# Attention beside the last stage ended sooner, and the last products of a seven-product scheme in another order

## Chip, cores and metric

One core of a Trainium2 chip. The metric is the device time of one execution in microseconds (us): the median of 3 runs, with the least and the greatest. Profile times are counted from the start of the profiled span.

## What is computed

Attention over a window, with a few global keys, and then a feed-forward block (ReGLU) on its result. Batch 4, 8 heads, 768 positions, head size 64; the feed-forward block takes 3072 tokens of width 512 through width 1536.

```python
def _attn_ref(q, k, v, n_global, n_local):          # n_global 8, n_local 96
    scores = scale * np.matmul(q, k.transpose(0, 1, 3, 2))
    is_global = pos[None, :] < int(n_global)
    is_local = (rel >= 0) & (rel < int(n_local))
    keep = is_global | is_local
    ...
    scores = np.where(keep, scores + bias, -1000000000.0)
    a = np.exp(scores - np.max(scores, axis=-1, keepdims=True))
    a = a / (np.sum(a, axis=-1, keepdims=True) + 1e-09)
    return np.matmul(a, v)

def _moe_ref(x, w_gate, w_val, w_out):              # x: the attention's result
    gate = np.maximum(x @ w_gate, 0.0)
    val = x @ w_val
    return (gate * val @ w_out).astype(np.float32)
```

## The kernel before

The 3072 tokens are worked in eight halves of 384 (half a batch item each), c = 0 to 7. The feed-forward block of half c and the attention of half c + 1 go through the engines together: the code makes a list of feed-forward items and a list of attention pieces, and `weave` lays the pieces between the items. Every engine takes its own instructions in the order in which the code gives them out.

For half c the feed-forward items are, for each of 12 slices of the width 1536, a gate (4 matmuls, then a ReLU on ScalarE) and a val (4 matmuls, then a product on VectorE, which writes `ht`), and then the output products:

```python
def gate(fc, ...):
    psg = products(f"g{fc % 4}", wg, fc, d0, d1)          # 4 matmuls 128x384, lhsT = wg, rhs = xT
    ...
    nc.scalar.activation(gr, psg[:, 0:QH], AF.Relu, bias=0.0, scale=1.0)

def val(fc, ...):
    psv = products("v", wv, fc, d0, d1)
    ...
    nc.vector.tensor_tensor(ht[:, fc, :], psv[:, 0:QH], st["r", fc], op=ALU.mult)
```

The attention of a half has 30 pieces (some of them empty, called `wait`): three units of scores, each in four PSUM banks, twelve exponentials with masks, and for each of four pairs of heads two AV products (5 matmuls each) with the normalisation: on ScalarE a logarithm `lnd` after each AV and one exponential `rcp` for both, on VectorE two products, which write a quarter of `xT`. The next half's gates read `xT`.

```python
return (X(U[0]) + X() + X() + X() + wait + X(U[1]) + X() + X() + a0[0:1] + X() + a0[1:2] + N(0) + wait
        + X(U[2]) + X() + a1[0:1] + X() + X() + a1[1:2] + N(1) + wait * 2 + AV(2) + N(2) + wait * 2
        + AV(3) + N(3))
```

```python
def spread(items, first, last):
    n = len(items)
    return [(first + (i + 0.5) / n * (last - first), f) for i, (_, f) in enumerate(items)]

for c in range(2, NHALF):                                  # NHALF = 8
    placed = []
    if c + 1 < NHALF:
        placed.append(spread(attention_pieces(c + 1), 0.0, 0.92))
    ...
    f1, f2 = ffn_pieces(c)
    weave(f1 + f2, *placed)
```

The output products of two blocks of 128 tokens are taken together by a scheme of seven half-size products in place of eight (Strassen's, in Winograd's form): `Pair`. Each product is 6 matmuls 128x256. Products 1 to 7 read `ht`, sums of it (`ss`), weights (`bb`) or differences of weights (`tt`); sums on VectorE put the four result blocks together in `obuf`. For c = 6 the items are p1, p2, p4, p6, p5, p7, p3. The very last pair is split differently, so that blocks can be stored one by one:

```python
def p1():                                                  # P1
    self.product(bank("b"), 0, hh(0, 0), bb(0, 0))
    st["o"] = obuf[:, n_results[0] % 2]
    nc.scalar.copy(st["o"][:, 2], st["b"][:, 0:DH])
def p2():                                                  # P2
    self.product(bank("a"), 0, hh(0, 1), bb(1, 0))
def p6():                                                  # o0 = P1 + P2 and o1 = P1 + P6
    self.product(st["a"], DH, ss(2), tt(2))
    add(st["o"][:, 0:2], two(st["a"]), st["o"][:, 2:3].to_broadcast([128, 2, DH]))
def block(t, d, i):                                        # store block i
    store(t, st["o"][:, i : i + 1], d, d + 1)
def onto(i, key, j):                                       # o_i = product + o_j
    add(st["o"][:, i], st[key][:, 0:DH], st["o"][:, j])
def last6():
    p6()
    block(0, 0, 0)
def last4():
    self.product(bank("4"), 0, hh(1, 1), tt(4))
    onto(2, "4", 1)
def last7():
    self.product(bank("7"), 0, ss(3), tt(3))
    onto(2, "7", 2)
    block(1, 0, 2)
    onto(3, "7", 1)
def last5():
    self.product(bank("5"), 0, ss(1), tt(1))
    onto(3, "5", 3)
    block(1, 1, 3)
    onto(4, "5", 1)
def last3():
    self.product(bank("3"), 0, ss(4), bb(1, 1))
    onto(4, "3", 4)
    block(0, 1, 4)
...
    return [(0.65, f) for f in (p1, p2, last6, last4, last7, last5, last3)]
```

PSUM is used through three pools: two banks for AV (and the first bank of each score unit), three for scores, three for the feed-forward products (`ff_ps`).

Of the kernel before, what the change touches and what calls it, by code (L numbers as in the profile page):

```python
# [16 lines left out]
def kernel(  # L17
# [27 lines left out]
    NHALF = 2 * B  # L45
# [450 lines left out]
    def score_unit(s, groups, pools):  # L496


        b, half = divmod(s, 2)
        out = []  # L500
        for pp, g in groups:
            banks = []
            for e in range(2):
                pool, name = pools.pop(0)
                banks.append(pool.tile([128, 512], FP32, name=name))
                out.append((pp, g, e, banks[e]))
            c = 0
            for j, a, w, m in banks_of_half[half][g]:
                for p in (2 * pp, 2 * pp + 1):
                    for e in range(2):  # L510
                        r = slice(64 * e, 64 * e + 64)
                        q3 = qT2[s % 2][r, p].rearrange("d (n p) -> d n p", n=NN)
                        nc.tensor.matmul(banks[e][:, c : c + NN * w], lhsT=kT[b % 2][p][r, j, :],  # L513
                                         rhs=q3[:, :, a : a + w], start=True, stop=True)
                    c += NN * w
        return out

    def unit_exp(s, pp, g, e, ps):
        bank = banks_of_half[s % 2][g]
        cols = sum(2 * NN * w for _, _, w, _ in bank)  # L520
        es = es_pool.tile([128, 480], BF16, name="es")
        nc.scalar.activation(es[:, 0:cols], ps[:, 0:cols], AF.Exp, bias=0.0, scale=scale)  # L522

        def mask():
            c = 0
            for j, a, w, m in bank:
                n_ = 2 * NN * w
                e4 = es[:, c : c + n_].rearrange("k (i n p) -> k i n p", i=2, n=NN)
                h0 = 4 * pp + e
                mk = m_all[:, h0 : h0 + 3 : 2, 0 if j == 0 else 1, :, m : m + w]  # L530
                if w == WQ:
                    e4 = e4.rearrange("k i n p -> k i (n p)")
                    mk = mk.rearrange("k i n p -> k i (n p)")
                nc.vector.tensor_mul(e4, e4, mk)  # L534
                for i in range(2):
                    es_of[s, 2 * pp + i, j, e] = (es, c + i * NN * w)
                c += n_

        return mask

    def attention_pieces(s):
        masks, units = [], []

        def flush():
            for f in masks:
                f()
            masks.clear()

        def scores(groups, pools):
            units.extend(score_unit(s, groups, list(pools)))  # L550

        def x(scored=None):
            ready = masks[:]
            masks.clear()
            if scored:
                scores(*scored)
            masks.append(unit_exp(s, *units.pop(0)))
            for f in ready:
                f()

        U = [([(0, 0), (0, 1)], (AVB, QKB, QKB, QKB)),
             ([(0, 2), (1, 0)], (AVB, QKB, QKB, QKB)),
             ([(1, 1), (1, 2)], (AVB, QKB, QKB, QKB))]
        X = lambda u=None: [(0.0, lambda: x(u))]
        AV = lambda p: [(0.0, lambda e=e: (flush(), piece_av(s, p, e))) for e in range(2)]
        N = lambda p: [(0.0, lambda: piece_norm(s, p, 1))]
        wait = [(0.0, lambda: None)]
        a0, a1 = AV(0), AV(1)
# [4 lines that stand above are left out]
# [30 lines left out]
    class Pair:  # L603
# [31 lines left out]
        def items(self, between=(), split=False):  # L635

            st = {}
            between = dict(between)
            hh = lambda t, f: lambda i: self.h(t, f, i, i + 1)[:, 0]
            ss = lambda n: lambda i: self.s[n][:, i]  # L640
            bb = lambda f, d: lambda i: B(i, i + 1, f, d)[:, 0]
            tt = lambda n: lambda i: T(n, i, i + 1)[:, 0]
            add = lambda o, x, y: nc.vector.tensor_tensor(o, x, y, op=ALU.add)  # L643
            two = lambda ps: ps.rearrange("p (b d) -> p b d", b=2)

            def bank(key):
                st[key] = ff_psum.tile([128, DM], FP32, name="ff_ps")
                return st[key]

            def store(t, blocks, d0=0, d1=2):  # L650
                c, n = self.tiles[t]
                nc.sync.dma_start(out=two(out_v[c, n])[:, d0:d1], in_=blocks)


            def p1():
                self.product(bank("b"), 0, hh(0, 0), bb(0, 0))
                st["o"] = obuf[:, n_results[0] % 2]
                n_results[0] += 1
                nc.scalar.copy(st["o"][:, 2], st["b"][:, 0:DH])

            def p2():
                self.product(bank("a"), 0, hh(0, 1), bb(1, 0))

            def p4():
                self.product(bank("d"), 0, hh(1, 1), tt(4))

            def p6():
                self.product(st["a"], DH, ss(2), tt(2))
                add(st["o"][:, 0:2], two(st["a"]), st["o"][:, 2:3].to_broadcast([128, 2, DH]))

            def p5():
                self.product(st["d"], DH, ss(1), tt(1))
                add(st["o"][:, 2:4], two(st["d"]), st["o"][:, 1:2].to_broadcast([128, 2, DH]))

            def second(ps):
                add(st["o"][:, 1:5:3], ps.unsqueeze(1).to_broadcast([128, 2, DH]), st["o"][:, 2:4])
                store(1, st["o"][:, 1:5:3])

            def p7():
                self.product(bank("c"), 0, ss(3), tt(3))  # L680

            def p3():
                self.product(st["c"], DH, ss(4), bb(1, 1))
                second(st["c"][:, 0:DH])
                add(st["o"][:, 3], st["c"][:, DH:], st["o"][:, 3])
                store(0, st["o"][:, 0:4:3])

            def block(t, d, i):  # L690
                store(t, st["o"][:, i : i + 1], d, d + 1)

            def onto(i, key, j):
                add(st["o"][:, i], st[key][:, 0:DH], st["o"][:, j])

            def last6():
                p6()
                block(0, 0, 0)

            def last4():  # L700
                self.product(bank("4"), 0, hh(1, 1), tt(4))
                onto(2, "4", 1)

            def last7():
                self.product(bank("7"), 0, ss(3), tt(3))
                onto(2, "7", 2)
                block(1, 0, 2)
                onto(3, "7", 1)

            def last5():  # L710
                self.product(bank("5"), 0, ss(1), tt(1))
                onto(3, "5", 3)
                block(1, 1, 3)
                onto(4, "5", 1)

            def last3():
                self.product(bank("3"), 0, ss(4), bb(1, 1))
                onto(4, "3", 4)
                block(0, 1, 4)

            def item(name, f):
                def g():
                    f()
                    for x in between.get(name, ()):
                        x()
                return (0.65, g)

            if split:
                return [(0.65, f) for f in (p1, p2, last6, last4, last7, last5, last3)]
            return [item(*x) for x in (("1", p1), ("2", p2), ("4", p4), ("6", p6), ("5", p5), ("7", p7), ("3", p3))]  # L730

    def ffn_pieces(c):
# [73 lines left out]
# [4 lines that stand above are left out]
# [28 lines left out]
    def AV(s, p, *pools):  # L838
        piece_av_wide(s, p, *pools)
        piece_norm_wide(s, p)  # L840
# [155 lines left out]
    for c in range(2, NHALF):  # L996
        placed = []
        if c + 1 < NHALF:
            placed.append(spread(attention_pieces(c + 1), 0.0, 0.92))
        if c + 2 < NHALF:  # L1000
            load_qk(c + 2, 0, H)
            load_v_half(c + 2)
            placed.append(spread(early_pieces(c + 2), 0.25, 0.75))
        f1, f2 = ffn_pieces(c)
        weave(f1 + f2, *placed)
# [35 lines left out]
```

The softmax here doesn't subtract the row's maximum and nothing guards it: scores larger than these inputs give would overflow.

## Time and profile before

| | |
|---|---|
| time, median of 3 runs | 240.92 us (240.51 to 241.19) |
| span of the profiled run | 239.0 us |
| TensorE (PE) busy | 229.8 us, 96% |
| VectorE (DVE) busy | 173.7 us, 73% |
| ScalarE (ACT) busy | 149.5 us, 63% |
| GpSimd (POOL) busy | 90.3 us, 38% |
| granted TensorE clock | 1.0 |
| bytes read and written in HBM | 28.38 MB and 6.29 MB |

How to read the profile: "L742" is line 742 of the kernel. L742 is a matmul of a gate or val, L632 one of the seven products, L431 of an AV, L513 of scores; L440 is the logarithm and L445 the exponential of the normalisation, L451 its product; L751 is the ReLU, L758 the product that writes `ht`; L522 and L534 are exponential and mask of the scores; L643 is a sum onto `obuf`, L652 a store. A name after the engine is the tile written. The chain of work that ended last is followed back from the last instruction, at each step to what released it; "issue" is time in which an engine waited for nothing that the profile shows. The end of a matmul in the profile is modelled, and matmuls overlap, so what is read here is the distance of their starts. Idle time of an engine that isn't the bottleneck costs nothing.

### The profile page before, as it was taken

To read this page: it belongs to the slowest core of one execution; us is meant where nothing else is said; L and a number is where in the kernel's file an instruction comes from. 1 tells how busy PE (TensorE), PEld (TensorE's weight loads), DVE (VectorE), ACT (ScalarE), POOL (GpSimd) and SP (SyncE) were. 2 spreads that over 40 slices of the span, in tenths; PEclk is the share of its full clock that TensorE was granted. 3 is DMA by queue.
4 is the path that set the end of the run, shared out by engine and by line. 5 is a ranking of instruction groups with operands and counts; after the bars stand their busy time and mean duration, and the time that the engine had idled before them with its cause. 6 is when DMAs were issued, how large, how long until landed. Compare 5 with 4: busy or idle time off the path is not lost.

```text
span 239.0 us, 5383 instructions
## 1 busy us (share of the span) xinstructions
PE 229.8 (96%) x1967; PEld 152.4 (64%) x1967; DVE 173.7 (73%) x443; ACT 149.5 (63%) x324; POOL 90.3 (38%) x191
## 2 busy tenths in 40 slices
PE   6889999999999999999999999999999999999992
PEld 3676656656458566766658566766658666756682
DVE  6878667756778779396866879496866878664783
ACT  6999756568653787657754787657754787433300
POOL 8998804925194067303491066402450000000000
PEclk9999999999999999999999999999999999999999
DMA  6999999997459943928349754919321200020004
GB/s 171 200 181 185 205 290 252 161 101 256 101 167 126 310 101 86 96 90 264 89 59 117 244 162 89 93 56 299 81 54 44 91 0 0 3 88 0 3 27 150
DMA packets 70650, 30.42 MB, mean 127 GB/s; under 512 B 47744, under 2 KB 69248, under 8 KB 70624
## 3 DMA queue, kind: packets, MB, share of 16 engines
q0 software_dynamic: 34896, 10.27, 38.2%
q1 hardware_dynamic: 35728, 19.82, 28.5%
q8 instruction: 15, 0.25, 0.4%
q14 instruction: 11, 0.09, 0.1%
HBM read 28.38 MB, written 6.29 MB: 145 GB/s over the span
## 4 chain that ended last, share of the span: by engine, by line
PE 81%; ACT 6%; DMA 6%; DVE 3%; POOL 1%; issue 1%; SPq 0%; DVEq 0%
PE ff_ps L742 49%; PE ff_ps L632 14%; PE ff_ps L775 9%; PE av_ps L431 5%; DMA wv<-in_moe_w_val_dram 4%; PE av_ps L513 2%; PE qk_ps L513 2%; ACT es L359 2%; DMA qs<-in_q_dram 1%; POOL vbuf L154 1%; ACT obuf L263 1%; ACT lnd L440 1%; DVE obuf L643 1%; DVE xT L451 1%; ACT rcp L445 1%
## 5 line engine op out<-in xcount | busy, mean ns | idle before, releaser
L742 PE MATMUL ff_ps<-xT,wg 128*128 128x384 bf16 x384 | 77.9, 326 | 0.4 <-DVE xT L451 0.4
L742 PE MATMUL ff_ps<-xT,wv 128*128 128x384 bf16 x384 | 77.9, 326 | 0.1
L751 ACT ACTIVATE grelu<-ff_ps 128x384 bf16<-128x384 f32 x96 | 46.8, 490 | 47.2 <-PE ff_ps L742 34.2
L758 DVE TENSOR_TENSOR ht<-ff_ps,grelu 128x384 f16<-128x384 f32 x96 | 53.3, 556 | 27.3 <-PE ff_ps L742 24.0
L742 PEld LDWEIGHTS <-wv 128*128 128x128 bf16 x384 | 36.1, 98 | 24.3 <-issue 1.7
L742 PEld LDWEIGHTS <-wg 128*128 128x128 bf16 x384 | 36.4, 98 | 21.9 <-issue 0.7
L451 DVE TENSOR_TENSOR xT<-av_ps,rcp 64x384 bf16<-64x384 f32 x48 | 26.6, 554 | 22.2 <-ACT rcp L445 21.1
L440 ACT ACTIVATE lnd<-av_ps 64x384 f32<-64x384 f32 x48 | 23.3, 485 | 17.8 <-PE av_ps L431 17.1
L367 POOL CAST kc<-ks 128x384 bf16<-128x384 f32 x20 | 10.2, 553 | 55.5 <-DMA ks<-in_k_dram 48.1
L534 DVE TENSOR_TENSOR es<-es,m_all 128x432 bf16<-128x432 bf16 (+3 forms) x108 | 30.3, 321 | 0.8 <-ACT es L522 0.7
L522 ACT ACTIVATE es<-qk_ps 128x432 bf16<-128x432 f32 (+2 forms) x54 | 27.8, 530 | 0.1
L154 POOL DMA_DIRECT2D vbuf<-in_v_dram x29 | 24.8, 870 | 0.3 <-DVE ht L758 0.3
L775 PE MATMUL ff_ps<-wo_sb,ht 128*128 128x512 f16 x96 | 23.6, 378 | 0.0
L643 DVE TENSOR_TENSOR obuf<-ff_ps,obuf 128x512 f32<-128x512 f32 (+1 forms) x35 | 20.4, 589 | 3.4 <-PE ff_ps L632 0.8
L431 PEld LDWEIGHTS <-vbuf 128*128 128x128 bf16 x216 | 18.3, 98 | 6.7
L431 PE MATMUL av_ps<-es,vbuf 128*128 128x216 bf16 (+4 forms) x216 | 21.4, 226 | 0.0
L632 PEld LDWEIGHTS <-hsum 128*128 128x128 f16 x168 | 16.2, 98 | 1.8
L632 PEld LDWEIGHTS <-ht 128*128 128x128 f16 x144 | 13.8, 98 | 3.4 <-DVE ht L758 0.8
L632 PE MATMUL ff_ps<-wo_sum,hsum 128*128 128x256 f16 x126 | 15.0, 272 | 0.0
L775 PEld LDWEIGHTS <-ht 128*128 128x128 f16 x96 | 8.6, 97 | 8.0 <-issue 0.6
L445 ACT ACTIVATE rcp<-lnd 128x384 f32<-128x384 f32 x24 | 12.5, 523 | 0.8
L632 PE MATMUL ff_ps<-wo_sb,ht 128*128 128x256 f16 x96 | 12.0, 273 | 0.5 <-DVE ht L758 0.5
(130 smaller groups left out, 252.7 us busy)
## 6 DMA issues: line engine op xcount, KB each, us to landing
out_dram<-obuf SPq DMA_DIRECT2D x22, 256.0 KB
ks<-in_k_dram SPq DMA_DIRECT2D x5, 768.0 KB
qs<-in_q_dram SPq DMA_DIRECT2D x5, 768.0 KB
vbuf<-in_v_dram POOLq DMA_DIRECT2D x23, 120.0 KB, 4.7
wv<-in_moe_w_val_dram POOLq DMA_DIRECT2D x3, 512.0 KB, 10.0
wo_sb<-in_moe_w_out_dram POOLq DMA_DIRECT2D x1, 1536.0 KB, 21.7
wg<-in_moe_w_gate_dram POOLq DMA_DIRECT2D x2, 512.0 KB, 10.0
ks<-in_k_dram SPq DMA_DIRECT2D x4, 192.0 KB
```

The costliest lines, as they stand in the source:

```text
L154: nc.gpsimd.dma_start(out=v_dst(b, NG + r0, NG + r0 + n, j), in_=v[b, :, KT * j + r0 : KT * j + r0 + n, :].rearrange("h p d -> p h d"))
L431: nc.tensor.matmul(av3[:, :, a : a + w], lhsT=vb[:, j, z0 : z0 + 128], rhs=es[:, c : c + NN * w].rearrange("k (n p) -> k n p", n=NN), star ...
L440: nc.scalar.activation(ln[o0 : o0 + 64], av[d0 : d0 + 64, 0:QH], AF.Ln, bias=0.0, scale=1.0)
L451: nc.vector.tensor_tensor(xT_of[s][r, p, :], av_of[s, p, e][r, 0:QH], av_of[s, p, "r"][r], op=ALU.mult)
L522: nc.scalar.activation(es[:, 0:cols], ps[:, 0:cols], AF.Exp, bias=0.0, scale=scale)
L534: nc.vector.tensor_mul(e4, e4, mk)
L632: nc.tensor.matmul(ps[:, c0 : c0 + DH], lhsT=lhs(i), rhs=rhs(i), start=(i == 0), stop=(i == NP - 1), skip_group_check=True)
L643: add = lambda o, x, y: nc.vector.tensor_tensor(o, x, y, op=ALU.add)
L742: nc.tensor.matmul(st[key][:, 0:QH], lhsT=w_of(w, dc, fc), rhs=xT_of[c][:, dc, :], start=(dc == 0), stop=(dc == N_DC - 1))
L751: nc.scalar.activation(gr, psg[:, 0:QH], AF.Relu, bias=0.0, scale=1.0)
L758: nc.vector.tensor_tensor(ht[:, fc, :], psv[:, 0:QH], st["r", fc], op=ALU.mult)
L775: nc.tensor.matmul(ps2, lhsT=ht[:, fc, n * 128 : (n + 1) * 128], rhs=wo_sb[:, fc, :], start=(fc == 0), stop=(fc == N_FC - 1))
```

## The change

There are two parts. The first lets the pieces of the last half's attention (c = 6, the attention of half 7) run to 87 per cent of the stage in place of 92; it is to have the normalisations done before the products that follow them. The other stages keep 0.92. The second gives the last pair's products the order 1, 2, 6, 5, 7, 4, 3 and forms P5 + o1 once, for two blocks; it is to leave a single sum behind the last product.

```diff
+            def last5():
+                self.product(bank("5"), 0, ss(1), tt(1))
+                onto(4, "5", 1)
+
+            def last7():
+                self.product(bank("7"), 0, ss(3), tt(3))
+                onto(3, "7", 4)
+                block(1, 1, 3)
+                onto(2, "7", 1)
+
             def last4():
                 self.product(bank("4"), 0, hh(1, 1), tt(4))
-                onto(2, "4", 1)
-
-            def last7():
-                self.product(bank("7"), 0, ss(3), tt(3))
-                onto(2, "7", 2)
+                onto(2, "4", 2)
                 block(1, 0, 2)
-                onto(3, "7", 1)
-
-            def last5():
-                self.product(bank("5"), 0, ss(1), tt(1))
-                onto(3, "5", 3)
-                block(1, 1, 3)
-                onto(4, "5", 1)
...
-                return [(0.65, f) for f in (p1, p2, last6, last4, last7, last5, last3)]
+                return [(0.65, f) for f in (p1, p2, last6, last5, last7, last4, last3)]
...
-            placed.append(spread(attention_pieces(c + 1), 0.0, 0.92))
+            placed.append(spread(attention_pieces(c + 1), 0.0, 0.92 if c + 2 < NHALF else 0.87))
```

## The prediction

> **What bounds the kernel now.** I read the page's busy shares first, then the chain of work that ended last in order of time, then the timelines of TensorE (PE), ScalarE (ACT) and VectorE (DVE) where that chain leaves PE, and last the order of instructions in the two built programs.
>
> ```profile
> PE 229.8 (96%) x1967; PEld 152.4 (64%) x1967; DVE 173.7 (73%) x443; ACT 149.5 (63%) x324; POOL 90.3 (38%) x191
> PEclk9999999999999999999999999999999999999999
> ```
>
> PE is busy 96% of the span at full clock. The change removes no product, so it can only win where PE stands still or has already finished. The chain in order of time (start, us, what) shows both places, at the end of the stage with the last attention beside it and at the end of the program:
>
> ```profile
> 202.50 0.49 ACT grelu L751
> 203.01 0.49 ACT lnd L440
> 203.53 0.53 ACT rcp L445
> 204.06 0.02 issue
> 204.08 0.55 DVE xT L451
> 204.63 0.48 DVE ht L758
> 205.11 0.04 issue
> 205.15 0.94 PE ff_ps L632 x7
> ```
>
> The timelines of DVE and PE at the same place (start, us, what; in brackets the idle time before and what ended it):
>
> ```profile
> 204.56 0.54 DVE L758 TENSOR_TENSOR ht<-ff_ps,grelu 128x384 f16<-128x384 f32 x1
> 205.15 0.28 PE L632 MATMUL ff_ps<-wo_sb,ht 128*128 128x256 f16 x1 [0.54 <-DVE ht L758]
> ```
>
> The first wait. Twelve output products (p1, p2) start at 203.25, 0.109 us apart (six take 0.655), so the twelfth is due at 203.25 + 11 x 0.109 = 204.45. It starts at 205.15: **0.70 us lost**. It needs the last slice of ht. The inputs of that slice were ready at 202.99 (grelu, 202.50 + 0.49) and about 203.4 (val), but DVE first ran a normalisation (L451) that waited for ACT's ln and exp of the third pair of heads. The same happens once more for the fourth pair, again in the chain:
>
> ```profile
> 207.91 0.53 ACT rcp L445
> ...
> 209.64 0.57 DVE xT L451
> 210.21 0.04 issue
> 210.25 15.36 PE ff_ps L742 x93
> ```
>
> The next stage's first gate begins at 209.16; its products stand 0.162 apart, so its fourth, which reads the fourth slice of xT, is due at 209.64. It starts at 210.25: **0.61 us lost**. Two smaller gaps: the third unit of scores starts at 194.36 where 194.18 was due (0.18: its PSUM bank comes free with a normalisation), and the second gate of the next stage 0.09 late, at 211.15. In all 0.70 + 0.61 + 0.18 + 0.09 = 1.58 us of waiting in this stretch; after 211.15 PE runs without a gap up to the last product.
>
> ```profile
> 225.61 9.18 PE ff_ps L632 x84
> 234.80 0.01 issue
> 234.81 0.77 DVE obuf L643 x2
> 235.58 0.03 issue
> 235.60 0.02 DVEq L643
> 235.63 0.04 issue
> 235.67 0.42 DVE obuf L643
> ```
>
> The tail. PE ends at 234.80, yet three DVE sums follow, the last at 235.67 to 236.09. Its store is issued at 236.12 and the span ends at 238.98: 2.86 us that the change does not touch.
>
> **What the Trainium skill says.** "Perfetto Trace Analysis", Tensor Engine Instruction: ACT and DVE are strict FIFO, and PE's end times are modelled. The trace agrees with the first: ht waited for an xT it does not use. "Perfetto Trace Analysis", Matmuls: independent groups should rotate through PSUM banks so that one is emptied while the next fills; the gap at 194.36 is a bank not yet emptied. "VectorE: DVE Perf Modes", The DRAIN you can't avoid: a dependent DVE instruction needs a semaphore, which is said to cost nothing. The trace differs. Independent 128x256 sums start 0.34 apart (233.95, 234.29); a dependent one started 0.52 after the one before it (234.29 to 234.81), 0.10 after its end. "DMA: Bandwidth & Descriptors", Anatomy of one DMA: about 2 us fixed, most of it completion. That page speaks of the GpSimd path; here 2.86 us pass from the last issue to the end, closing steps included, and I carry this over.
>
> **Part one, 0.87 for 0.92.** Nothing is added or removed; the 30 attention pieces of the last half are spread over less of the stage's 31 items (12 gates, 12 vals, 7 output products of some 0.65 us each), a piece at the end of the list by 0.05 x 31 = 1.5 items. By the order of PE instructions in the built programs, the first and the third score unit and the second AV of pair 0 keep their places; the second score unit, the first AV of pair 0 and the AVs of pairs 1 and 2 come one item earlier, those of pair 3 two. AV of pair 2 used to end one val before p1 and now ends a gate and a val before it. AV of pair 3 stood after p4 and p6, and now stands after p1 and p2.
>
> The twelfth product. I follow pair 2 through after's order, with ACT's steps as the trace has them (ln 0.49, exp 0.52, grelu 0.49, 0.03 between), on before's clock. Its second AV ends at 202.76 today; one item (0.65) and some 0.15 regained further up make it 201.95; ln to 202.47, exp to 203.02, and grelu of the last slice, which after has behind them, to about 203.45. DVE does two normalisations 0.58 apart from 203.05, then ht, 0.47 after the second one starts, from 204.1 to 204.64. The twelfth product, which now has an AV (0.31) ahead of it, is due at 204.45 + 0.31 - 0.15 = 204.61, and can start some 0.05 after ht: 204.70. So 0.1 to 0.15 stays: **gain 0.55**.
>
> The fourth gate product. Pair 3's second AV ends at 207.36 today; two items (1.31) and the 0.70 regained above make it 205.35. Its ln and exp take it to 206.42, two normalisations to 207.59. The gate's fourth product, due today at 209.64, will be due near 208.95. That wait is gone: **gain 0.6**. But in after's DVE order both sums that empty the PSUM banks of p2 and p4 stand behind these normalisations: 207.62 to 208.31 and, 0.10 later, 208.41 to 209.08. The next stage's first gate and first val wait for just these banks and are due near 208.5 and 209.15. It is nearly a tie; I leave 0.1 for it, in exchange for the 0.09 of today.
>
> Score units. The third should find its bank in time, as its norm comes 0.2 to 0.3 earlier (0.18 back). The second now comes one val earlier, at 187.76. It needs four PSUM banks, and the last is freed by the exp that ends at 187.98, so its fifth product waits 0.1 to 0.15. Net **+0.05**, and a gate whose bank is the one just used may lose 0.05 more at 199.8. Sum of part one: 0.55 + 0.6 + 0.05 = **1.2 us**.
>
> **Part two, the order of the last pair.** Before: product 6, 4, 7, 5, 3, and six 128x256 sums; after: 6, 5, 7, 4, 3, and five, as P5+o1 is formed once and read by two blocks. In before's clock PE ends product 6 at 232.16 and the four others 0.655 apart: 232.82, 233.48, 234.13, 234.79. DVE's sums, at 0.10 after a dependency and 0.34 between independent starts: the wide sum of 6 to 232.95; 5 from 233.05 to 233.48; 7 from 233.58 and 233.92, to 234.34; 4 from 234.44 to 234.86; the last waits for product 3 alone: 234.88 to 235.30. Its start moves from 235.67 to 234.88: 0.79. One thing is not explained: today the first sum of product 7 starts at 233.95, though its inputs were there at 233.48. Should this delay recur for product 7, the last sum starts at 235.15 and the gain is 0.52. I take **0.65**. Stores: two of the last three now come 0.43 apart in place of 0.86; the issue takes 0.33, so they don't queue at issue.
>
> **The sum.** 1.2 + 0.65 = 1.85, off 240.92: 239.07; I write **239.0**.
>
> **Rivals.** (1) Attention is held by its own ACT and DVE chain: pieces put earlier on PE only wait there. For it: the second score unit, and ACT's 8.98 us busy of 10 between 190 and 200. Against: ACT is busy 5.19 of 12 from 200 to 212, where the two large waits lie. Then the tail alone is left, with half of the rest: 239.7. (2) The wait moves from xT to the PSUM banks at the start of the next stage, because sums stand behind normalisations. For it: the tie above. Against: at the end of the stage DVE has nothing else. It would take 0.3 to 0.6 back: 239.5. (3) The last two stores share the DMA engines and completion grows, hiding the tail's gain. Against: a 128 KB store moves in under 0.5 us at the 380 GB/s that the trace shows near 233.5. It would cost 0.2 to 0.4: 239.3.
>
> **Range and chances.** With all waits gone and the full tail: 1.58 + 0.79, about 238.5. With rivals (1) and (2) in part: 239.7. Runs of before spread 0.68 us, so I widen a little: 238.4 to 239.8. Two per cent is 4.8 us, while all the waiting that the change can reach is under 2.5. So within 2% is nearly sure.
>
> **What would show it.** In the profile after: the twelfth output product at most 0.2 late; no wait for xT at the first gate of the last stage; a fifth product of the second score unit that waits some 0.1; last DVE sum within 0.2 of PE's end, and 2.9 from the store to the end. I am wrong if the first gate or val of the last stage waits over 0.3 for a bank, if ht still comes 0.5 late, or if the last store lands later.

## The result, and the profile after

| | before | after |
|---|---|---|
| time, median of 6 runs each, us | 241.07 (240.51 to 241.96) | 239.50 (239.00 to 240.28) |
| ratio after / before | | 0.9932, 95% interval 0.9906 to 0.9958 |
| span of the profiled run, us | 238.98 | 237.76 |

The change makes the kernel 0.7% faster: 1.57 us by the medians, where 1.85 was predicted. The busy shares on the page of after show the same work (the mean granted clock was 0.999 of full speed). Line numbers move by a line or two between the kernels: L742 of before is L741 in after and L743 in best, L758 is L757.

```profile
PE 230.5 (97%) x1967; PEld 152.6 (64%) x1967; DVE 174.1 (73%) x442; ACT 149.5 (63%) x324; POOL 90.1 (38%) x191
```

PE has as many instructions as before (1967), DVE one fewer (the sum that is now shared). The gain lies in the gaps.

**A clock for comparing runs.** The start of the stage with the last attention moves from run to run (the first score product was at 184.53 us in before's trace, 184.74 in after's, 184.11 to 184.94 in the others), although nothing ahead of it was changed. Counted from that product, traces of kernels with the same code up to a point agree within 0.005 us there. So I count from it. "Second val" is the second val of the next stage; from there to the last matmul every kernel takes 22.71 us. As in the prediction, a counted product (first, twelfth, fourth) is one matmul; a numbered one (p1, product 7) is six. Every time given for a group is that of its first matmul; "last matmul" is the sixth of product 3.

| us from the stage's first score product | before | after | gain |
|---|---|---|---|
| first output product (p1) | 18.721 | 18.701 | 0.020 |
| twelfth output product (when it was due) | 20.623 (19.922) | 20.458 (20.207) | |
| first gate of the next stage | 24.628 | 24.157 | 0.471 |
| its fourth product | 25.725 | 24.645 | 1.080 |
| second val of the next stage | 27.273 | 26.196 | 1.077 |
| last matmul of the program (its start) | 49.983 | 48.907 | 1.076 |
| end | 54.448 | 53.025 | 1.423 |

So 1.08 us come from part one and 0.35 from the tail. The chain of work that ended last in after (start, us, what) shows where time is still lost:

```profile
202.00 0.32 PE av_ps L431 x5
...
202.34 0.49 ACT lnd L440
...
202.85 0.53 ACT rcp L445
...
203.41 0.26 DVE xT L451
...
203.99 0.56 DVE xT L451
...
204.58 0.57 DVE ht L757
...
205.19 0.28 PE ff_ps L632
...
209.06 15.69 PE ff_ps L741 x96
224.75 9.18 PE ff_ps L632 x84
...
233.94 0.42 DVE obuf L643
```

The twelfth output product (205.19) still waits for ht, and ht for the same normalisation, though less than in before. The second large wait, of the next stage's first gate for xT, has left the chain: from 205.48 on it is PE alone up to the tail. The timeline of PE around the next stage's start (start, us, what) says so product by product:

```profile
208.89 0.81 PE L741 MATMUL ff_ps<-xT,wg 128*128 128x384 bf16 x4
209.60 0.81 PE L741 MATMUL ff_ps<-xT,wv 128*128 128x384 bf16 x4
210.29 0.81 PE L741 MATMUL ff_ps<-xT,wg 128*128 128x384 bf16 x4
```

A group of four products takes 0.65 from its start to the next. The first gate's four now stand together (before, the fourth stood apart, behind a wait of 0.61). What is left is 0.06 ahead of the first val (0.71 from 208.89 to 209.60), which starts 0.05 after the end (209.55) of the sum that empties the bank of p4 and p5, and 0.035 ahead of the second gate. Further up, PE's timeline of after shows the score units and a gate:

```profile
187.97 0.26 PE L513 MATMUL av_ps<-qT,kT 64*128 64x216 bf16 x1
...
188.54 0.82 PE L741 MATMUL ff_ps<-xT,wv 128*128 128x384 bf16 x4
...
199.49 0.81 PE L741 MATMUL ff_ps<-xT,wv 128*128 128x384 bf16 x4
200.23 0.81 PE L741 MATMUL ff_ps<-xT,wg 128*128 128x384 bf16 x4
```

The second score unit takes 0.57 (187.97 to 188.54) where it took 0.51 in before: 0.07 lost. The gate at 200.23 comes 0.09 late (0.74 after the val). The third unit's 0.18 of before is gone. The losses of after, 0.07 + 0.09 + 0.25 + 0.06 + 0.035, are 0.50 against 1.58: a difference of 1.08, which is the shift of the second val.

The tail, by the timelines of DVE and of SyncE's queue (SPq, the issue of stores) in after (in brackets the idle time before and what ended it):

```profile
231.39 1.22 DVE L643 TENSOR_TENSOR obuf<-ff_ps,obuf 128x512 f32<-128x512 f32 x2 [0.18 <-PE ff_ps L632]
233.08 1.62 DVE L643 TENSOR_TENSOR obuf<-ff_ps,obuf 128x256 f32<-128x256 f32 x4 [0.47 <-DVE obuf L643]
```

```profile
234.40 0.33 SPq L652 DMA_DIRECT2D out_dram<-obuf  x1
...
234.82 0.38 SPq L652 DMA_DIRECT2D out_dram<-obuf  x1
```

Before had three sums behind the last product. After has two, since the first sum of product 7 starts only at 233.08, after an idle time of 0.47, and pushes the sum of product 4 (233.94) past PE's end. The last sum ends at 234.70; its store is issued 0.12 later, as SyncE is busy with the store before it until 234.73.

### The profile page after: what moved, and what is told of

The parts are those of the page before. It is cut to its first block, busy times and chain, and to the rows that moved or that the text cites. A ratio compares the mean times of both kernels' runs of the same rounds, so it can differ in the third digit from the quotient of the medians.

```text
span 237.8 us, 5381 instructions
## 1 busy us (share of the span) xinstructions
PE 230.5 (97%) x1967; PEld 152.6 (64%) x1967; DVE 174.1 (73%) x442; ACT 149.5 (63%) x324; POOL 90.1 (38%) x191
## 4 chain that ended last, share of the span: by engine, by line
PE 84%; POOL 7%; DMA 4%; issue 1%; DVE 1%; ACT 0%; DVEq 0%; POOLq 0%
PE ff_ps L741 50%; PE ff_ps L632 15%; PE ff_ps L774 9%; PE av_ps L431 6%; DMA wv<-in_moe_w_val_dram 4%; POOL vbuf L154 3%; PE av_ps L513 2%; PE qk_ps L513 2%; POOL kc L131 1%; POOL wg L171 1%; POOL qT L195 1%; PE qk_ps L299 1%; DVE xT L451 0%; POOL wv L171 0%; DVE ht L757 0%
## 5 line engine op out<-in xcount | busy, mean ns | idle before, releaser
L741 PE MATMUL ff_ps<-xT,wv 128*128 128x384 bf16 x384 | 77.9, 326 | 0.3 <-DMA wv<-in_moe_w_val_dram 0.3
L741 PE MATMUL ff_ps<-xT,wg 128*128 128x384 bf16 x384 | 77.8, 326 | 0.0
L757 DVE TENSOR_TENSOR ht<-ff_ps,grelu 128x384 f16<-128x384 f32 x96 | 53.3, 556 | 27.6 <-PE ff_ps L741 24.0
L741 PEld LDWEIGHTS <-wv 128*128 128x128 bf16 x384 | 36.0, 98 | 24.2 <-issue 1.1
L741 PEld LDWEIGHTS <-wg 128*128 128x128 bf16 x384 | 36.3, 97 | 22.0 <-issue 0.7
```

Of the source, the lines that this page charges most:

```text
L741: nc.tensor.matmul(st[key][:, 0:QH], lhsT=w_of(w, dc, fc), rhs=xT_of[c][:, dc, :], start=(dc == 0), stop=(dc == N_DC - 1))
```

## Experiments

Times below are from the same stage clock. "Tail" is the time from the start of the last matmul (the sixth of product 3) to the end of the span: 4.465 in before, 4.118 in after. Where a ratio is given, it is against runs of before on the same chip, with its 95% interval; the kernels without one were run once and are read by their traces alone.

**1. Part one alone, part two alone.** Do they add, and which is worth what?

```diff
 # p1_only, from before
-            placed.append(spread(attention_pieces(c + 1), 0.0, 0.92))
+            placed.append(spread(attention_pieces(c + 1), 0.0, 0.92 if c + 2 < NHALF else 0.87))
 # p2_only, from after
-            placed.append(spread(attention_pieces(c + 1), 0.0, 0.92 if c + 2 < NHALF else 0.87))
+            placed.append(spread(attention_pieces(c + 1), 0.0, 0.92))
```

> Part one alone (0.87 in the last stage, the last pair in the old order). Theory: the whole gain is waiting that TensorE no longer does, and the two parts lie one after the other and simply add. Then the stretch from the last stage's first scores to the third gate or val of the stage after it is about 1.08 us shorter than before, and the tail from the last product's last matmul to the end of the span is as before (4.46 us): in all about 1.1 us, ratio near 0.9955. Rival, that attention is held by its own ScalarE and VectorE chain and only the tail was won: no more than 0.4 us, and the twelfth output product still 0.5 us late or more.

> Part two alone (0.92 everywhere, the last pair in the new order). Theory: the waits of the last stage are as before (twelfth output product 0.70 us late, fourth gate product 0.61 us late), and the tail is some 0.35 us shorter: the last sum starts 0.5 us sooner after the last matmul, but its store is issued 0.12 us after the sum's end in place of 0.03, because the queue is still issuing the store before it. In all 0.3 to 0.4 us, ratio near 0.9985. Rival, that most of the change's gain is in the tail: 0.8 us or more.

| | second val | tail | end | time, us | ratio |
|---|---|---|---|---|---|
| part one alone | 26.194 | 4.460 | 53.365 | 239.85 | 0.9955 (0.9941 to 0.9968) |
| part two alone | 27.268 | 4.090 | 54.069 | 240.43 | 0.9976 (0.9963 to 0.9990) |

(Before ran at 240.97 beside them.) By the traces part one is worth 1.08 (54.448 - 53.365), part two 0.38 (54.448 - 54.069), and 1.46 is within 0.04 of the 1.42 of both together. The two parts hardly touch each other. With part two alone the twelfth product is again held as long as in before:

```profile
204.73 0.28 PE L632 MATMUL ff_ps<-wo_sb,ht 128*128 128x256 f16 x1 [0.54 <-DVE ht L757]
```

Rival (1), that attention is held by its own chain and only the tail is left, falls.

**2. Why is the twelfth product still 0.25 late?** DVE's timeline of after at that place, and the last ReLU from ACT's:

```profile
203.41 1.14 DVE L451 TENSOR_TENSOR xT<-av_ps,rcp 64x384 bf16<-64x384 f32 x2
204.58 0.56 DVE L757 TENSOR_TENSOR ht<-ff_ps,grelu 128x384 f16<-128x384 f32 x1
203.28 0.47 ACT L750 ACTIVATE grelu<-ff_ps 128x384 bf16<-128x384 f32 x1
```

The inputs of ht were there by 203.75 (the end of its ReLU; its val ended at 203.60 by the modelled ends). The two normalisations start at 203.407 and 203.989; ht starts at 204.580, which is 0.59 after the second one's start and 0.03 after its end (204.549). My prediction had 0.47 after the start. The second normalisation works on partitions 64 to 127, and ht starts at partition 0. The Trainium skill, "VectorE: DVE Perf Modes", section "Two Vector instructions with no wait between them", gives it as a model that an instruction is held until all earlier VectorE instructions have finished when an input or its output starts in another group of 32 partitions than the last one in the same memory (SBUF or PSUM). In norm_after_ht the two normalisations have ht between them, so ht stands behind the one that starts at partition 0 as it does. Pair 2's pieces for the second normalisation come two places later, in the last half alone:

```diff
-                + X(U[2]) + X() + a1[0:1] + X() + X() + a1[1:2] + N(1) + wait * 2 + AV(2) + N(2) + wait * 2
-                + AV(3) + N(3))
+                + X(U[2]) + X() + a1[0:1] + X() + X() + a1[1:2] + N(1) + wait * 2 + AV(2)
+                + (N(2) + wait * 2 if s < NHALF - 1 else wait * 2 + N(2)) + AV(3) + N(3))
```

> The changed kernel, with the second normalisation product of the third pair put behind the last val, so that VectorE runs: first normalisation product (partitions 0 to 63), ht (from partition 0), second normalisation product (from partition 64). Theory: in the changed kernel ht waited until the second normalisation product had ended, because an instruction that starts at another partition isn't begun before the one in front of it ends; so the twelfth output product was 0.25 us late. Here ht starts 0.47 to 0.48 us after the first normalisation product's start, and the twelfth output product is less than 0.05 us late: 0.2 to 0.25 us less than the changed kernel. Rival, that ht waited for its own inputs (ReLU and val): ht starts no sooner and the lateness stays near 0.25 us.

DVE's timeline in this kernel, and PE's:

```profile
203.24 0.55 DVE L451 TENSOR_TENSOR xT<-av_ps,rcp 64x384 bf16<-64x384 f32 x1
203.71 0.54 DVE L757 TENSOR_TENSOR ht<-ff_ps,grelu 128x384 f16<-128x384 f32 x1
204.28 0.56 DVE L451 TENSOR_TENSOR xT<-av_ps,rcp 64x384 bf16<-64x384 f32 x1
```

```profile
204.23 0.82 PE L632 MATMUL ff_ps<-wo_sb,ht 128*128 128x256 f16 x6
```

Here ht starts 0.474 after the normalisation in front of it started, 0.07 before that one ended. The second normalisation, which starts at partition 64, begins 0.03 after ht's end. That agrees with the page both ways: held where the start partition changes, not held where it stays. All six products of p2 stand together, the twelfth at 20.208, on time. The second val comes at 25.964, 0.232 sooner than in after, and nothing later takes it back: the end is 52.781 against 53.025. Timed: 239.07, ratio 0.9932 (0.9914 to 0.9950); an interval this wide can't tell it from after's, the trace can. The gain of 0.23 has two causes here, one normalisation fewer ahead of ht and no hold, and this run does not part them. The hold by itself is the 0.12 between the 0.474 and the 0.59.

**3. What delays the first sum of product 7?** It is the delay that the prediction left unexplained. In after the sum before it ends at 232.61, its own wait instruction is done at 232.67, the sum starts at 233.08. It starts 0.48 after its product's modelled end; its neighbours start some 0.09 after theirs. Four theories: (a) it belongs to PE's running out of work, as product 7 has twelve products behind it; (b) it belongs to the PSUM bank; (c) it belongs to the store issued beside it (232.11, 0.34 long); (d) it belongs to the place in DVE's own row of instructions: counting its waits too, this sum is DVE's 577th instruction in after and in before. (That is the count in the built program. A branch at the program's start has no record in the trace, where the sum is the 576th record.) Each got an edit of its own.

```diff
 # pe_tail: twelve more matmuls behind the last product (nobody reads them)
                 block(0, 1, 4)
+                spare = qk_psum.tile([128, 512], FP32, name="qk_ps")
+                for _ in range(12):
+                    nc.tensor.matmul(spare[:, 0:DH], lhsT=wo_sb[:, 0, 0:128], rhs=B(0, 1, 0, 0)[:, 0], start=True, stop=True)
 # dve_shift: one small write more on DVE, before the last pair (p1); ident isn't read afterwards
+                if split:
+                    nc.vector.memset(ident[:, 0:2], 0.0)
 # p7_bank: product 7 into a bank of the scores' pool
-                self.product(bank("7"), 0, ss(3), tt(3))
+                st["7"] = qk_psum.tile([128, 512], FP32, name="qk_ps")
+                self.product(st["7"], 0, ss(3), tt(3))
 # late_store: the first block's store moved from last6 to last3, ahead of the last store
                 p6()
-                block(0, 0, 0)
 ...
                 onto(4, "3", 4)
+                block(0, 0, 0)
                 block(0, 1, 4)
```

> The changed kernel with twelve more 128x256 matmuls behind the last product, into a PSUM bank that nothing reads (1.3 us of TensorE, while the stores are still under way). Question: in both kernels the first sum of product 7 starts 0.48 us after that product's modelled end, where every other sum that waits for TensorE alone starts 0.09 us after it. Theory A, that the delay belongs to TensorE's reaching the end of its instructions (its closing instruction begins within 0.05 us of where that sum should start): with more matmuls behind, the sum of product 7 starts 0.09 to 0.10 us after the product or its dependency, and the last sum some 0.27 us sooner after the last product. Theory B, that it belongs to this sum, its bank or its place in VectorE's instructions: the delay of 0.38 us stays.

> The changed kernel with one small memset (128x2) more on VectorE ahead of the very last pair's first product; it writes a tile that nothing reads any more. It moves all later VectorE instructions one place on. The delay in question: the first sum of product 7 starts 0.48 us after that product's modelled end instead of 0.09 (0.38 us too late). Theory C, place in VectorE's instructions: the delay moves to the instruction in front, the sum of product 5, and the sum of product 7 follows 0.10 us after its dependency. Theory B, that it belongs to this product or its sum: it stays where it was, 0.38 us.

> The changed kernel with product 7 in a PSUM bank of the scores' pool, idle by then, in place of a bank of the feed-forward pool. Theory D, the PSUM bank: the sum of product 7 starts 0.09 to 0.10 us after the product's end or its dependency, and the last sum up to 0.27 us sooner after the last matmul. If the bank is not the cause the delay of 0.38 us stays.

> The changed kernel with the store of the pair's first block (the one that is issued just as product 5's sum starts, and moves while the sum of product 7 should start) issued at the very end instead, in front of the last store. Theory E, that the store's reading of the same buffer holds VectorE: the sum of product 7 starts without the 0.38 us. If the store is not the cause the delay stays. Either way the end of the program comes later, by the 0.38 us or so that one more issue in front of the last store takes.

The tail sums by DVE's timeline. First pe_tail, then p7_bank (late_store has 233.28 and 0.47, too):

```profile
233.28 1.62 DVE L643 TENSOR_TENSOR obuf<-ff_ps,obuf 128x256 f32<-128x256 f32 x4 [0.46 <-DVE obuf L643]
```

```profile
233.26 0.76 DVE L643 TENSOR_TENSOR obuf<-qk_ps,obuf 128x256 f32<-128x256 f32 x2 [0.47 <-DVE obuf L643]
```

The idle time stays at 0.46 to 0.47 with more work on PE, in another bank, and without the store. The last sum starts 0.624, 0.640 and 0.641 after the start of product 3's last matmul, as in after (0.642). Theories (a), (b) and (c) fall. (pe_tail was timed too: 239.29, ratio 0.9944, 0.9928 to 0.9961, which can't be told from after's.) Now dve_shift:

```profile
231.31 0.06 DVE L657 MEMSET ident<- 128x1 uint32 x1
231.54 2.99 DVE L643 TENSOR_TENSOR obuf<-ff_ps,obuf 128x512 f32<-128x512 f32 x6 [0.17 <-issue]
```

The six sums now run one after another without the long idle time, the last starts 0.309 after the last matmul does, and the tail is 3.748 in place of 4.118: one DVE instruction more, 0.37 us sooner. One thing in its expectation was missed: the delay was to move to the sum of product 5. But with one instruction more, the 577th is the wait ahead of product 7's sum. It comes 0.04 after the sum in front of it ends, as elsewhere; that a delay is hidden under that sum, which runs for 0.42, would fit but isn't shown. If (d) holds, a second write must put the delay on product 5's sum:

```diff
 # dve_shift2, on top of dve_shift
                     nc.vector.memset(ident[:, 0:2], 0.0)
+                    nc.vector.memset(ident[:, 2:4], 0.0)
```

> The changed kernel with two small memsets more on VectorE ahead of the very last pair's first product, where the run before had one. In the changed kernel the late sum of product 7 is VectorE's 577th instruction, the first after nine times 64; with one memset more the 577th is the wait ahead of that sum, and nothing was late. With two more it is the sum of product 5 itself. Theory C, that the delay belongs to the place in the row of instructions (here the first of a block of 64): now the sum of product 5 comes late, some 0.3 to 0.4 us after the wait in front of it instead of 0.04 to 0.05. Rival, that any instruction more in front of it removes the delay: nothing is late, as with one memset.

```profile
230.95 0.06 DVE L657 MEMSET ident<- 128x1 uint32 x1
230.96 0.06 DVE L658 MEMSET ident<- 128x1 uint32 x1
...
232.34 2.15 DVE L643 TENSOR_TENSOR obuf<-ff_ps,obuf 128x256 f32<-128x256 f32 x5 [0.47 <-DVE obuf L643]
```

It does. The idle 0.47 now stands ahead of product 5's sum, which starts 0.41 after its wait is done (231.925 to 232.339) where others take 0.045; it is 0.37 later than in after, and the tail is back at 4.117. So the delay is bound to the place in the row, and the sum that falls on it pays. All thirteen kernels of this case agree: in the ten with a sum at this place it starts 0.40 to 0.41 after its wait, and in the three with a wait there (dve_shift, f82, best) no sum of the tail does. What the engine does there isn't shown by these runs. The place is 9 x 64 + 1; an ht at the 193rd, 3 x 64 + 1, starts 0.40 after its wait too, though its inputs were there, but nothing of the kind is seen at the 129th and the 257th. A refill of instructions may come to mind. Yet the Trainium skill, "Runtime: NRT & Kernel Launch", section "Instruction fetch mechanics", has blocks of 256 instructions and calls the cost mostly hidden; 577 and 193 aren't such places, nor do blocks of 256 give two places 384 apart, and 0.37 us isn't hidden, so the page doesn't explain it, and I leave the cause open.

**4. The last store.** SyncE is still issuing one store when the last sum is done. act_store gives the last store to ScalarE's queue, which is idle there.

```diff
-            def store(t, blocks, d0=0, d1=2):
-                nc.sync.dma_start(out=two(out_v[c, n])[:, d0:d1], in_=blocks)
+            def store(t, blocks, d0=0, d1=2, eng=nc.sync):
+                eng.dma_start(out=two(out_v[c, n])[:, d0:d1], in_=blocks)
...
-                block(0, 1, 4)
+                block(0, 1, 4, nc.scalar)
```

> The changed kernel with its last store issued by ScalarE's queue in place of SyncE's. Theory: in the changed kernel the last store was issued 0.12 us after its sum in place of 0.03, as SyncE was still busy with the store before it; here it is issued 0.03 to 0.05 us after the sum, and the span from the last matmul's start to the end goes from 4.12 us to about 4.03. Rival, that the end is set by the landing of the store before it, or that the two stores share the DMA engines: the issue is sooner and the end is not.

The timeline of the two last issues in this kernel (ACTq is ScalarE's queue):

```profile
234.21 0.33 SPq L652 DMA_DIRECT2D out_dram<-obuf  x1
234.55 0.37 ACTq L652 DMA_DIRECT2D out_dram<-obuf  x1
```

The issue follows the last sum's end by 0.031 (0.120 in after), and the tail is 4.009, 0.109 shorter. late_store is the opposite case: three stores queue up, the last issue comes 0.61 after the last sum's end (1.664 against 1.055), and the tail is 4.626.

From the last issue to the end it is 2.85 in before and with part one alone, where the two last stores come 0.86 apart, and 2.93 to 2.96 in every kernel where they come 0.33 to 0.52 apart; some 0.05 of the difference is the last issue itself, 0.38 in after against 0.33.

**5. Is 0.87 the best place, and what do the three findings make together?** f82 puts 0.82 for 0.87. best is norm_after_ht, dve_shift and act_store in one.

> The changed kernel with 0.82 in place of 0.87. Theory: the two normalisations come still earlier, so that the twelfth output product is on time (0.25 us back), and the first gate and val of the next stage no longer wait; but the third score unit now comes one item earlier and waits 0.1 to 0.3 us for its PSUM bank, which the first pair's normalisation frees: within 0.15 us of the changed kernel either way. Rival, attention held by its own chain: the third score unit waits 0.4 us or more, and all the earlier placing is lost there.

> The changed kernel with the three things that the runs so far showed to help: the third pair's second normalisation product behind the last val, one small memset more on VectorE ahead of the last pair, and the last store issued by ScalarE's queue. Theory: the gains lie at different places of the chain and add, 0.24 + 0.37 + 0.05 (after the memset the two last stores are 0.5 us apart, so that ScalarE's queue has less left to save than the 0.11 it saved alone): from the last stage's first scores to the end about 52.35 us, against 53.02 of the changed kernel and 54.45 of the kernel before; ratio to the kernel before near 0.991. Rival, that the end is then set by the landing of the stores: less than 0.4 us of it arrives.

With 0.82 the twelfth product is on time (20.921; the first output product is itself 0.72 later, with one AV, 0.31, more ahead of it), but the third score unit pays for it, by PE's timeline:

```profile
192.62 0.81 PE L741 MATMUL ff_ps<-xT,wv 128*128 128x384 bf16 x4
193.86 0.24 PE L513 MATMUL av_ps<-qT,kT 64*128 64x192 bf16 x1 [0.43 <-DVE xT L451]
```

It comes 1.243 after the val, where after has 0.746 (194.460, after a gate at 193.714): 0.50 lost, as the rival had it, and more than the 0.25 of the twelfth product and the 0.09 of the gate at 200.23 that are won. The second val is at 26.345, 0.15 later than with 0.87. f82's end is sooner all the same (52.804), but only since its number of DVE instructions ahead of product 7's sum is another and the delay of experiment 3 doesn't show (tail 3.748). That is luck, not the placing of the pieces.

best: twelfth product on time (20.207), second val 25.963, last sum 0.310 after the last matmul's start, last issue 0.031 after that sum's end, tail 3.692, end 52.366. That is 0.66 sooner than after (0.23 + 0.37 + some 0.06 of the store). Timed: 238.87 (238.30 to 239.72, 6 runs) beside 240.93 of before, ratio 0.9923 (0.9901 to 0.9945). This overlaps after's interval; that it beats after is shown by the traces, not by the times. The chain that ended last is, from the fourth pair's last AV on, now PE alone to 230.85:

```profile
205.41 3.27 PE ff_ps L632 x30
208.69 15.69 PE ff_ps L743 x96
224.38 6.47 PE ff_ps L632 x60
```

## Why the prediction was right or wrong

The time, 239.5, lies in the range (238.4 to 239.8), and "within 2%" was right. The centre was 0.5 too low. By its own steps:

- **What bounds the kernel: right.** Only gaps of PE and the tail could give anything. Part one's gain is the difference of the gaps, 1.58 to 0.50, and nothing was given back later: 22.71 us from the second val to the last matmul in every kernel.
- **Twelfth output product, "gain 0.55": mechanism right, size off.** It gained 0.45 (0.70 to 0.25 late). The failed term is "then ht, 0.47 after the second one starts": 0.59 was measured, as ht is held behind an instruction that starts at partition 64, and it costs 0.12. The "0.15 regained further up" was 0.02 at the first output product, since the gate at 200.23 and the second score unit took most of it back; but ht and the product that waits for it were both shifted by nearly as much (0.15 and 0.13), so this matters little.
- **Fourth gate product, "gain 0.6": right.** 0.61.
- **The tie of the banks, "I leave 0.1", in exchange for 0.09: right.** The first gate waited for no bank, the first val 0.06, and 0.035 of the second gate's 0.09 stayed. Rival (2) is thereby answered: the wait doesn't move to the banks.
- **Score units, "net +0.05": nearly.** 0.18 back and 0.07 lost, and the gate at 199.8 (in before's clock), where 0.05 more was feared, lost 0.09: +0.02 in all. Part one came to 1.08 where the sum had 1.2.
- **The last sum, "I take 0.65": wrong branch.** The step named the right condition, "should this delay recur for product 7 ... the gain is 0.52", and split the difference. The delay recurred: the last sum's start gained 0.517 (1.159 to 0.642 after the last matmul's start). Without it, as dve_shift shows, it would have been 0.85 (1.159 to 0.309). The count of DVE instructions ahead of the sum, which the two built programs show, would have told that it stays on the same sum.
- **"So they don't queue at issue": wrong.** The step set the issue (0.33) against sums 0.43 apart. But the two sums end 0.33 apart (234.37 and 234.70), as the delay of product 7 makes them run back to back; and from one issue's start to the next it is 0.42 (234.40 to 234.82), so the queue isn't free in time: 0.09 lost.
- **"2.86 us that the change does not touch": off by 0.09.** It became 2.94, in step with the stores' distance, as rival (3) had it, but well under its "0.2 to 0.4", and about half of it is the longer last issue (0.38 for 0.33). Only the distance goes with it in these runs; the shared DMA engines as its cause are argued, not shown. 0.517 + 0.01 (a shorter last sum) - 0.09 - 0.09 = 0.35 is the tail's gain.
- **What was to be seen.** No wait for xT: so. A fifth score product that waits 0.1: 0.07. The first gate and val within 0.3 of their banks: so. The twelfth product at most 0.2 late: 0.25. The last sum within 0.2 of PE's end: it starts 0.37 after it.

In sum 1.08 + 0.35 = 1.42 by the traces in place of 1.85. The medians differ by 1.57; the 0.15 between them is small beside the interval of the ratio (some 1.0 to 2.3 us) and is not explained further.

## What to carry to other kernels

Before moving work in time, list for each wait not only who it waits for but in which order the engine takes its instructions and at which partition each begins: here ht, behind a normalisation that starts at partition 64, waited for its end, and putting ht between the two normalisations won 0.23 us. An unexplained delay in the profile of before should be tried by its own experiment (one small instruction more ahead of it), since splitting the difference put this prediction 0.13 us off, and a kernel that seems better for the placing of its pieces, as with 0.82, may only have moved the delay. At the end of a program, try the last store on a queue that isn't issuing another one: alone it won 0.11 us here.

## What was not expected of the hardware

- A sum at one fixed place in VectorE's row of instructions, the 577th of the built program, starts about 0.37 us late: a sum of product 7 in before and after, a sum of product 5 with two instructions more. With one more a wait stands there, and no sum is late. One memset of 0.06 us makes the tail 0.37 us shorter. Why is open.
- Of the normalisations and ht here, the one that starts at another partition than the one before it starts 0.03 after that one's end; the one that starts at the same partition started 0.474 after the start, 0.07 before the end. A change of partition isn't the only thing that does this: in before, a sum of ht that reads what the one in front of it wrote starts 0.03 after that one's end too (206.008 to 206.042), with no wait between them.
- The issue of a 128 KB store took its queue 0.33 to 0.42 us, and stores that queued up at the very end were issued 0.40 to 0.52 us apart (after, late_store). With the last one on ScalarE's queue the two issues came 0.33 apart and the last 0.03 after its sum.
